# Sliding-window attention and a two-layer feed-forward on one core: chunk 1's first layer ahead of chunk 0's second, two pairs of the third batch in tiles, V moved from two queues, and the last batch transposed on TensorE

## The chip, the cores and the metric

The kernel runs on one core of a Trainium2 chip. The metric is the device time of one execution in microseconds (us). An execution that was taken with a profile also shows its span, from the first to the last instruction of the core.

## The reference

q, k and v have the shape batch 8, heads 8, sequence 576, head size 64. Each position attends to itself and to the 63 positions before it. The result, 4,608 tokens of 512 values, goes through two matrices with `h - tanh(h)` between them. Cut to what is computed:

```python
scores = scale * np.matmul(q, k.transpose(0, 1, 3, 2))       # scale = 1/8
rel = pos[:, None] - pos[None, :]
mask = (rel >= 0) & (rel < 64)
scores = np.where(mask, scores, -1e9)
attn = np.exp(scores - np.max(scores, axis=-1, keepdims=True))
attn = attn / (np.sum(attn, axis=-1, keepdims=True) + 1e-9)
x = np.matmul(attn, v).transpose(0, 2, 1, 3).reshape(4608, 512)
h = x @ w_in                                                  # 512 x 2048
return (h - np.tanh(h)) @ w_out                               # 2048 x 512
```

## The kernel before, in words

**Attention.** Two heads make a pair; pair number g runs from 0 to 31, four to a batch (g = 4 x batch + pair). A sequence is cut into nine windows of 64 queries; each window looks at 128 keys, its own 64 and the 64 before. For each pair:

- q and k are loaded with a cast to bf16 (`load`, `load_all`; these DMAs are issued by POOL) and copied into rows in which the two heads lie side by side (`cast`, line 86, on VectorE or POOL).
- TensorE transposes them into PSUM, six transposes for each of q and k, and copies bring them to `qT` (or `qs`) and `kT`. There are two buffers of each (`g % NR`).
- The *wide* form (`tr`, `scores`, `masking`, `pv`, `norm`, lines 259 to 358) keeps q of the two heads in separate columns, with zeros in the other head's rows, so `qT` must have been cleared. ScalarE takes the exponential, VectorE multiplies with the mask, TensorE multiplies with V (which carries a column of ones, so the row sums come along), and VectorE divides.
- The *tile* form (`tr_rows`, `hides`, `tile_scores`, `tile_pv`, lines 278 to 324) works on half the rows of the array for each head. The mask is added by matmuls that write large negative numbers ahead of the scores (`hides`), and no mask is multiplied later. It needs one copy each for q and k.

Batches 0 and 1 use the tile form, batches 2 to 7 the wide one. V is loaded as 72 rows of eight positions, cast into `vb` (`cast_v`) and moved by nine DMAs to `vw`, in which window j has its 64 keys on the upper partitions (`keys_v`, or `windows_v` for both halves); `shift_dve` or `shift_v` copies them to the lower half of the next window. `vb` is single, `vw` is double.

In batch 7 of the kernel before, TensorE doesn't transpose q and k. POOL copies q to zeroed rows (`cast_q` to `qz`, cleared by `more_zeros`), SP writes q and k to DRAM (`bounce`) and reads them back with transposing DMAs into `qT` and `kT` (`tr_dma`).

The results of a batch, in `xs`, are transposed to `xT`, on TensorE (`x_tr`, half 0 or 1 being the pairs 0, 1 or 2, 3) up to batch 3, and by transposing DMAs (`x_dma`, SP) from batch 4 on.

**Feed-forward.** The 4,608 tokens are nine chunks of 512. A chunk has eight windows and a batch nine, so chunk c needs the batches up to c. For each of 16 slices m of 128 hidden units `hp_mm` runs four matmuls of 512 columns (line 396), ScalarE takes tanh (401), and VectorE subtracts into `gT` (`g_sub`, 408). The second layer, `yp_mm` (420), has 16 groups of four matmuls too: group st is a quarter of the sum for the 128 tokens s = st // 4. After four groups ScalarE copies the bank out (`y_out`, 425) and SP stores it. The first layer uses PSUM banks 0 to 2 for its first groups and then 0 and 1; the second layer uses bank 2, and in the last chunk banks 0 and 2.

**What sets the order.** The order on each engine is written by hand and kept. The program runs over slots h. A slot may hold one group of the feed-forward (table `OPS`), and anything else is hung on a slot by `at(h, fn, ...)`:

```python
OPS[2 * m] = "h", 0, m
OPS[32 + 2 * m] = "h", 1, m
OPS[49 + 2 * m if m < 8 else 56 + m] = "y", 0, m
for c in range(2, NC + 1):
    if c < NC:
        OPS[32 * c + 8 + 2 * m] = "h", c, m
    OPS[32 * c + 9 + 2 * m] = "y", c - 1, m
```

In a slot the group's matmuls come first, then what hangs on the slot, then the subtraction of the group. A slot costs no time by itself. Each engine takes its own instructions in this order, and one that waits holds up all behind it. For a pair in the wide form a number a (`STEPS`, or a formula) sets its places: casts of q and k at a - 7 and a - 5, transposes at a and a + 2, scores at a + 5, a + 7 and a + 9, mask at a + 11, products with V at a + 13 to a + 15, norm at a + 15. `LOADS` holds the slots of the loads of a batch (k, q, V) and `VALUES` those of V's casts and moves. Before each of these loads, POOL copies one element of the newest `gT` (`pace`, the `tick` of line 453), which keeps it from running ahead.

DMAs issued by POOL share eight completion semaphores in turn, so that one waits until the eighth before it has landed. Row buffers for casts are three deep for q and for k, `vall` is single, `qall` and `kall` are double.

Ahead of the loop stand batch 0 and the loads of batch 1's pairs and of `w_in`. `w_out` is loaded from slot 27.

Of the kernel before, what the change touches and what calls it, by code (L numbers as in the profile page):

```python
# [15 lines left out]
def kernel(  # L16
# [9 lines left out]
    nc = tc.nc  # L26
# [24 lines left out]
    dram = ctx.enter_context(tc.tile_pool(name="dram", bufs=2, space=bass.MemoryType.DRAM))  # L51
# [24 lines left out]
    qz = [const.tile([P, 2, E, 128], BF16, name=f"qz{i}") for i in range(2)]  # L76
# [40 lines left out]

    def cast_q(g):

        i = stage.pop((g, "q")).rearrange("p h (e d) -> p h e d", d=D)  # L120
        for h in range(2):
            nc.gpsimd.tensor_copy(qz[g % 2][:, h, :, 64 * h:64 * h + 64], i[:, h])

    def bounce(g, n):

        if n == "q":
            t = dram.tile([2, S, 128], BF16, tag="q", name="qd")
            nc.sync.dma_start(out=t.rearrange("h (p e) c -> p h (e c)", e=E),
                              in_=qz[g % 2].rearrange("p h e c -> p h (e c)"))
        else:  # L130
            t = dram.tile([S, 128], BF16, tag="k", name="kd")
            nc.sync.dma_start(out=t.rearrange("(p e) c -> p (e c)", e=E),
                              in_=rows.pop((g, "k")).rearrange("p e h d -> p (e h d)"))
        rows[g, n + "d"] = t

    def tr_dma(g, n):
        t = rows.pop((g, n + "d"))
        if n == "q":
            nc.sync.dma_start(out=qT[g % NR].rearrange("c h s -> c (h s)"),
                              in_=t.rearrange("h s c -> (h s) c"), transpose=True)  # L140
        else:
            nc.sync.dma_start(out=kT[g % NR][:, 64:], in_=t, transpose=True)
# [89 lines left out]

    def more_zeros(i):
        nc.gpsimd.memset(qz[i], 0.0)
# [175 lines left out]
    def yp_bank(c, s):  # L410
        if c == 0:
            return 2
        return (0, 2)[s % 2] if c == NC - 1 else 2
# [16 lines left out]
    for m in range(M):  # L430
        OPS[2 * m] = "h", 0, m
        OPS[32 + 2 * m] = "h", 1, m
        OPS[49 + 2 * m if m < 8 else 56 + m] = "y", 0, m
        for c in range(2, NC + 1):
            if c < NC:
                OPS[32 * c + 8 + 2 * m] = "h", c, m
            OPS[32 * c + 9 + 2 * m] = "y", c - 1, m
# [89 lines left out]
    at(6, lambda: [cast_v(1, pr, V) for pr in range(NP)])  # L527
    at(7, lambda: [keys_v(1, j, (G, Y)[j % 2]) for j in range(NJ)])
    at(7, load_v_all, 2)
    for g in 8, 9, 10, 11:  # L530
        at(7, load, g, "k", G)
        at(7, load, g, "q", G)
    at(9, cast_pair, 4, V)
    at(11, cast_pair, 5, V)
    at(18, cast_pair, 6, V)
    at(20, cast_pair, 7, V)
    at(22, shift_dve, 1, 0, 4)
    for g, t, ka, qa, a, b in ((4, (11, 12, 13, 14), 6, 7, (4, 5), (6, 7)), (5, (14, 15, 15, 15), 2, 3, (4, 5), (6, 7)),
                             (6, (19, 20, 21, 22), 2, 3, (4, 5), (4, 5)), (7, (21, 22, 24, 25), 2, 3, (4, 5), (4, 5))):
        at(t[0], tr_rows, g, "k", ka, V)  # L540
# [3 lines left out]
    for pr in range(NP):  # L544
        at(24 + 2 * pr, tile_pv, 4 + pr, (6, 7))
    at(26, lambda: [cast_v(2, pr, V) for pr in range(NP)])
    at(27, lambda: nc.vector.memset(qT[1], 0.0))
    at(29, x_tr, 1, 0, 0, 4, 3, A)
    at(30, x_tr, 1, 0, 4, 9, 4, A)
    at(31, x_tr, 1, 1, 0, 4, 3, V)  # L550
    at(31, x_tr, 1, 1, 4, 9, 4, A)
    at(27, lambda: [keys_v(2, j, G) for j in range(NJ)])
    at(27, load_w_out, 0)
    at(27, load_w_out, 1)
    at(27, load_all, 3, "q")
# [109 lines left out]
```

The softmax here doesn't subtract the row's maximum and nothing guards it: scores larger than these inputs give would overflow.

## Time and profile before

| what | value |
|---|---|
| median of 13 runs | 366.15 us (361.32 to 369.68) |
| the profiled execution's own time | 366.46 us |
| its span | 364.7 us |
| mean granted TensorE clock in it | 0.956 |
| TensorE matmuls, busy | 326.2 us, 2,380 recorded |
| VectorE, ScalarE, POOL, busy | 202.9, 184.5, 104.3 us |
| first layer, line 396 | 576 matmuls, 152.2 us busy |
| second layer, line 420 | 576 matmuls, 145.8 us busy |
| DMA | 41.84 MB, 115 GB/s in the mean |

The busy time of a matmul in the profile contains its way through the array, so neighbours overlap; how long a group of matmuls keeps the engine is read from the distance of the starts, or from the chain of work that ended last. A row in order of time has its start, its duration, the engine, the line and the operation, the tiles, the number of instructions merged, and in brackets the idle time of the engine before it with what ended this. A row of the windows has the stretch, its length, and busy time and count of PE, its weight loads (PEld), VectorE (DVE), ScalarE (ACT) and POOL, then the granted clock, the busy share of the DMA engines and their GB/s.

### The profile page before, as it was taken

The numbers are of one execution on the slowest core, as the hardware profiler recorded it, in microseconds if no ns is written. First come the engines' busy times: TensorE is split into PE (matmuls) and PEld (weight loads), VectorE is DVE, ScalarE is ACT, GpSimd is POOL, SyncE is SP. The second block draws the span as 40 slices with busy tenths as digits, with TensorE's granted clock in tenths as the row PEclk, the third lists the DMA queues.
The fourth block names the chain that finished last, engine by engine and source line by source line (L and its number), as shares of the span: only waits on it lengthen the run. The fifth ranks groups of instructions, "written<-read, shape, count | busy, mean of one in ns | idle before, by whom it ended". The sixth has DMA issues, their size and how long they took to land.

```text
span 364.7 us, 6139 instructions
## 1 busy us (share of the span) xinstructions
PE 326.2 (89%) x2380; PEld 178.3 (49%) x2380; DVE 202.9 (56%) x340; ACT 184.5 (51%) x336; POOL 104.3 (29%) x153
## 2 busy tenths in 40 slices
PE   6787785799879997999999999598999999999995
PEld 2553454355435554555555555154455444444442
DVE  4566578687534676567666686255556443344300
ACT  3533664656526564665656656254554443443421
POOL 8913707206104164652272260701000000000000
PEclk9559999889999999999999999899999999999999
DMA  8999985993059938946796779458940410011012
GB/s 160 161 193 179 167 126 66 175 202 81 29 101 153 154 64 141 148 89 107 161 150 140 139 112 133 115 132 179 200 131 31 94 54 33 29 42 45 30 59 85
DMA packets 50006, 41.84 MB, mean 115 GB/s; under 512 B 20873, under 2 KB 43337, under 8 KB 49785
## 3 DMA queue, kind: packets, MB, share of 16 engines
q0 software_dynamic: 21248, 19.34, 36.1%
q1 hardware_dynamic: 28376, 21.69, 26.0%
q10 hardware_dynamic: 352, 0.43, 0.4%
q8 instruction: 18, 0.29, 0.3%
q14 instruction: 12, 0.09, 0.1%
HBM read 36.70 MB, written 11.21 MB: 131 GB/s over the span
## 4 chain that ended last, share of the span: by engine, by line
PE 64%; DVE 10%; issue 8%; ACT 7%; DMA 6%; POOL 4%; ACTq 0%; SPq 0%; DVEq 0%; POOLq 0%
PE ps L420 28%; PE ps L396 26%; PE ps L346 3%; DVE xs L357 2%; PE ps L330 2%; DVE gT L408 2%; DMA w_out_sb<-in_moe_w_out_dram 2%; DMA kt<-kd 2%; DVE qt L86 2%; DMA vall<-in_v_dram 2%; ACT qt L84 1%; ACT th L401 1%; PE ps L263 1%; PE ps L363 1%; ACT pt L305 1%
## 5 line engine op out<-in xcount | busy, mean ns | idle before, releaser
L396 PE MATMUL ps<-xT,wi 128*128 128x512 bf16 x576 | 152.2, 389 | 3.6 <-DVE gT L408 2.0
L408 DVE TENSOR_TENSOR gT<-ps,th 128x512 bf16<-128x512 f32 x144 | 98.7, 690 | 96.9 <-ACT th L401 95.3
L420 PE MATMUL ps<-w_out_sb,gT 128*128 128x512 bf16 x576 | 145.8, 381 | 2.9 <-ACT ysb L425 2.8
L401 ACT ACTIVATE th<-ps 128x512 f32<-128x512 f32 x144 | 85.8, 598 | 92.1 <-PE ps L396 91.0
L396 PEld LDWEIGHTS <-wi 128*128 128x128 bf16 x576 | 61.4, 115 | 51.4 <-issue 8.3
L420 PEld LDWEIGHTS <-gT 128*128 128x128 bf16 x576 | 54.0, 98 | 58.0 <-issue 5.0
L332 ACT ACTIVATE pt<-ps 128x384 bf16<-128x384 f32 x72 | 35.2, 490 | 38.9 <-PE ps L330 38.8
L357 DVE TENSOR_TENSOR xs<-ps,rc 64x576 bf16<-64x576 f32 x48 | 36.2, 755 | 1.2
L425 ACT ACTIVATE ysb<-ps 128x512 f32<-128x512 f32 x36 | 21.5, 597 | 17.2 <-PE ps L420 17.2
L86 DVE COPY qt<-ps 64x576 bf16<-64x576 bf16 x20 | 15.2, 760 | 21.6 <-ACT qt L84 21.6
L86 POOL COPY vb<-vall 72x1024 bf16<-72x1024 bf16 x20 | 20.8, 1056 | 22.6 <-DMA vall<-in_v_dram 21.0
L346 PEld LDWEIGHTS <-pt 128*128 128x128 bf16 x216 | 18.2, 99 | 18.4 <-DVE pt L336 2.5
L330 PE MATMUL ps<-qt,kt 128*128 128x128 bf16 x216 | 24.3, 222 | 1.8 <-DMA kt<-kd 1.8
L346 PE MATMUL ps<-vw,pt 128*128 128x130 bf16 x216 | 24.2, 223 | 1.6 <-DVE pt L336 1.6
L86 POOL COPY qb<-qall 96x768 bf16<-96x768 bf16 x16 | 13.3, 828 | 29.6 <-DMA qall<-in_q_dram 25.1
L330 PEld LDWEIGHTS <-kt 128*128 128x128 bf16 x216 | 16.7, 99 | 9.9 <-DMA kt<-kd 2.2
L336 DVE TENSOR_TENSOR pt<-pt,ps 128x1152 bf16<-128x1152 bf16 x24 | 17.9, 745 | 0.1
L86 POOL COPY kb<-kall 96x768 bf16<-96x768 bf16 x20 | 16.6, 832 | 2.0 <-ACT pt L332 2.0
L84 ACT ACTIVATE kt<-ps 128x576 bf16<-128x576 bf16 x20 | 13.0, 650 | 7.7 <-PE ps L263 7.7
L176 POOL DMA_DIRECT2D vw<-vb x19 | 12.2, 655 | 11.7 <-DVE gT L408 8.1
L263 PE MATMUL ps<-ident,kb 96*128 96x96 bf16 x120 | 8.6, 209 | 6.3 <-POOL kb L86 4.3
L84 ACT ACTIVATE qt<-ps 64x576 bf16<-64x576 bf16 x20 | 12.7, 633 | 0.3 <-PE ps L263 0.3
(73 smaller groups left out, 193.4 us busy)
## 6 DMA issues: line engine op xcount, KB each, us to landing
out_dram<-ysb SPq DMA_DIRECT2D x36, 256.0 KB
vall<-in_v_dram POOLq DMA_DIRECT2D x7, 576.0 KB, 10.5
qall<-in_q_dram POOLq DMA_DIRECT2D x5, 576.0 KB, 9.7
kall<-in_k_dram POOLq DMA_DIRECT2D x5, 576.0 KB, 8.6
vw<-vb SPq DMA_DIRECT2D x35, 65.0 KB
vw<-vb SPq DMA_DIRECT2D x16, 130.0 KB
wi<-in_moe_w_in_dram POOLq DMA_DIRECT2D x2, 1024.0 KB, 15.5
w_out_sb<-in_moe_w_out_dram POOLq DMA_DIRECT2D x2, 1024.0 KB, 12.4
```

What stands on the lines that cost most here:

```text
L84: nc.scalar.activation(o, i, ACT.Copy)
L86: eng.tensor_copy(o, i)
L330: nc.tensor.matmul(sp[:, i, :], kT[g % NR][:, 64 * j:64 * j + 128], qT[g % NR][:, :, 64 * j:64 * j + 64], start=True, stop=True)
L332: nc.scalar.activation(PT[g % NPT][:, 3 * grp:3 * grp + 3, :], sp, ACT.Exp, scale=scale)
L336: nc.vector.tensor_tensor(p, p, mask.unsqueeze(1).to_broadcast([128, 2 * NJ, 64]), ALU.mult)
L346: nc.tensor.matmul(ps[:, 5 + grp, 130 * i:130 * i + 130], PT[g % NPT][:, j, :], vw[b % 2][:, j, 2 * pr:2 * pr + 2, :], start=True, stop=True)
L357: nc.vector.tensor_tensor(xo[r, :, :, pr, :], ov[r, :, :, h, 0:D], rc[r].to_broadcast([64, 3, 3, 64]), ALU.mult)
L396: nc.tensor.matmul(hp, w_in_tile(ki, m), chunk_tile(c)[:, :, ki % 2, 64 * (ki // 2):64 * (ki // 2) + 64], start=(ki == 0), stop=(ki == 3))
L401: nc.scalar.activation(th, hp, ACT.Tanh)
L408: nc.vector.tensor_tensor(gT[c][:, m, :], hp, th, ALU.subtract)
L420: nc.tensor.matmul(yp, gT[c][:, m, s * 128:(s + 1) * 128], w_out_sb[:, m, :], start=(m == 0), stop=(m == M - 1))
L425: nc.scalar.activation(ysb, ps[:, yp_bank(c, s), :], ACT.Copy)
```

## The change

The edit has four parts and what follows from them:

- The second layer of chunk 0 goes to slots 64 to 79, one group to a slot, behind all of chunk 1's first layer, and uses PSUM banks 0 and 1 in turn. Everything from chunk 2 on stands eight slots later. The first group of each chunk takes half 0 of its input before half 1.
- Batch 1's steps among slots 6 to 31 are respaced: casts of pairs 4 and 5 stand before V's cast, which goes from slot 6 to 11 (with its moves and the loads behind them from 7 to 12). k of pairs 6 and 7 is copied by ScalarE instead of VectorE.
- Pairs 8 and 9 of batch 2 use the tile form, at slots 29 to 48, among chunk 1's first layer. V of batch 2 and pairs 8 to 11 are cast by POOL instead of VectorE; V's moves for batch 2, and for batch 3, are issued by POOL and SP in turn. `w_out` is loaded from slot 23.
- Batch 7 is treated as batches 3 to 6: q and k are cast by POOL at a - 7 and a - 5 and transposed on TensorE. `qz`, `cast_q`, `bounce`, `tr_dma` and `more_zeros` go.

The diff, cut to its core:

```diff
-    qz = [const.tile([P, 2, E, 128], BF16, name=f"qz{i}") for i in range(2)]
...
     def yp_bank(c, s):
         if c == 0:
-            return 2
+            return s % 2
         return (0, 2)[s % 2] if c == NC - 1 else 2
...
-        OPS[49 + 2 * m if m < 8 else 56 + m] = "y", 0, m
+        OPS[64 + m] = "y", 0, m
         for c in range(2, NC + 1):
             if c < NC:
-                OPS[32 * c + 8 + 2 * m] = "h", c, m
-            OPS[32 * c + 9 + 2 * m] = "y", c - 1, m
+                OPS[32 * c + 16 + 2 * m] = "h", c, m
+            OPS[32 * c + 17 + 2 * m] = "y", c - 1, m
...
-    at(6, lambda: [cast_v(1, pr, V) for pr in range(NP)])
-    at(7, lambda: [keys_v(1, j, (G, Y)[j % 2]) for j in range(NJ)])
-    at(7, load_v_all, 2)
+    at(3, lambda: nc.vector.memset(qT[1], 0.0))
+    at(8, cast_pair, 4, V)
+    at(9, cast_pair, 5, V)
+    at(11, lambda: [cast_v(1, pr, V) for pr in range(NP)])
+    at(12, lambda: [keys_v(1, j, (G, Y)[j % 2]) for j in range(NJ)])
+    at(12, load_v_all, 2)
     for g in 8, 9, 10, 11:
-        at(7, load, g, "k", G)
-        at(7, load, g, "q", G)
-    at(9, cast_pair, 4, V)
-    at(11, cast_pair, 5, V)
-    at(18, cast_pair, 6, V)
-    at(20, cast_pair, 7, V)
-    at(22, shift_dve, 1, 0, 4)
-    for g, t, ka, qa, a, b in ((4, (11, 12, 13, 14), 6, 7, (4, 5), (6, 7)), (5, (14, 15, 15, 15), 2, 3, (4, 5), (6, 7)),
-                             (6, (19, 20, 21, 22), 2, 3, (4, 5), (4, 5)), (7, (21, 22, 24, 25), 2, 3, (4, 5), (4, 5))):
-        at(t[0], tr_rows, g, "k", ka, V)
+        at(12, load, g, "k", G)
+        at(12, load, g, "q", G)
+    at(16, cast_pair, 6, V)
+    at(18, cast_pair, 7, V)
+    at(21, shift_dve, 1, 0, 4)
+    for g, t, ka, qa, a, b, eng in ((4, (10, 11, 13, 14), 6, 7, (4, 5), (6, 7), V),
+                                    (5, (13, 14, 15, 15), 2, 3, (4, 5), (6, 7), V),
+                                    (6, (17, 18, 20, 21), 2, 3, (4, 5), (4, 5), A),
+                                    (7, (19, 20, 23, 24), 2, 3, (4, 5), (4, 5), A),
+                                    (8, (29, 30, 34, 36), 3, 2, (4, 5), (4, 5), A),
+                                    (9, (36, 37, 41, 43), 3, 2, (4, 5), (4, 5), A)):
+        at(t[0], tr_rows, g, "k", ka, eng)
         at(t[1], tr_rows, g, "q", qa, A)
...
-        at(24 + 2 * pr, tile_pv, 4 + pr, (6, 7))
-    at(26, lambda: [cast_v(2, pr, V) for pr in range(NP)])
-    at(27, lambda: nc.vector.memset(qT[1], 0.0))
-    at(29, x_tr, 1, 0, 0, 4, 3, A)
-    at(30, x_tr, 1, 0, 4, 9, 4, A)
-    at(31, x_tr, 1, 1, 0, 4, 3, V)
+        at(22 + 2 * pr, tile_pv, 4 + pr, (6, 7))
+    at(27, x_tr, 1, 0, 0, 4, 3, A)
+    at(28, x_tr, 1, 0, 4, 9, 4, A)
+    at(30, x_tr, 1, 1, 0, 4, 7, V)
     at(31, x_tr, 1, 1, 4, 9, 4, A)
-    at(27, lambda: [keys_v(2, j, G) for j in range(NJ)])
-    at(27, load_w_out, 0)
-    at(27, load_w_out, 1)
-    at(27, load_all, 3, "q")
-    at(27, load_all, 3, "k")
-    at(27, load_v_all, 3)
-    at(41, shift_dve, 2, 0)
-    at(42, shift_dve, 2, 4)
-    at(100, more_zeros, 0)
-    at(116, more_zeros, 1)
+    at(21, lambda: [cast_v(2, pr) for pr in range(NP)])
+    at(22, cast_pair, 8, G)
+    at(23, lambda: [keys_v(2, j, (G, Y)[j % 2]) for j in range(NJ)])
+    at(23, load_w_out, 0)
+    at(23, load_w_out, 1)
+    at(23, load_all, 3, "q")
+    at(23, cast_pair, 9, G)
+    at(23, load_all, 3, "k")
+    at(23, load_v_all, 3)
+    at(24, cast_pair, 10, G)
+    at(38, cast_pair, 11, G)
+    at(40, shift_dve, 2, 0, 4)
+    at(43, tile_pv, 8, (6, 7))
+    at(48, tile_pv, 9, (6, 7))
+    at(51, x_tr, 2, 0, 0, 4, 4, V)
+    at(52, x_tr, 2, 0, 4, 9, 5, A)
+    at(76, x_tr, 2, 1, 0, 4, 3, V)
+    at(78, x_tr, 2, 1, 4, 9, 3, A)
...
-    LOADS = {4: (74, 75, 77), 5: (101, 104, 97), 6: (132, 136, 119), 7: (156, 160, 150)}
-    STEPS = {2: (30, 38, 46, 54), 3: (63, 70, 77, 84), 4: (91, 98, 105, 112), 5: (119, 126, 134, 142)}
-    XTR = {9: (58, 60), 11: (70, 71), 13: (88, 90), 15: (100, 102)}
-    VALUES = {3: (64, 1, 68), 4: (84, 1, 90), 5: (107, 2, 115), 6: (124, 5, 142), 7: (156, 5, 174)}
-    for g in range(2 * NP, B * NP):
+    LOADS = {4: (75, 77, 79), 5: (106, 109, 102), 6: (140, 144, 126), 7: (168, 171, 158)}
+    STEPS = {2: (0, 0, 49, 58), 3: (72, 79, 86, 93), 4: (100, 107, 114, 121), 5: (128, 135, 142, 149)}
+    TURNS = {13: (97, 3, 99, 3), 15: (110, 4, 111, 3)}
+    VALUES = {3: (66, 1, 71), 4: (88, 1, 93), 5: (110, 2, 120), 6: (132, 5, 150), 7: (164, 5, 182)}
+    for g in range(2 * NP + 2, B * NP):
         b, pr = divmod(g, NP)
-        a = STEPS[b][pr] if b in STEPS else 8 * g - 44
-        if b == 2:
-            at((28, 33, 41, 49)[pr], cast_pair, g, V)
-        elif b == 7:
-            at(a - 14, cast_q, g)
-            at(a - 13, cast, g, "k")
-            at(a - 12, bounce, g, "q")
-            at(a - 11, bounce, g, "k")
-            at(a - 6, tr_dma, g, "q")
-            at(a - 5, tr_dma, g, "k")
-        else:
+        a = STEPS[b][pr] if b in STEPS else 8 * g - 36
+        if b > 2:
             at(a - 7, cast, g, "q")
             at(a - 5, cast, g, "k")
-        if b < 7:
-            at(a, tr, g, "q", 2 if g < 10 else 3, A, V)
-            at(a + 2, tr, g, "k", 2 if g < 10 else 3, A)
+        at(a, tr, g, "q", 2 if g < 13 else 3, A, V)
+        at(a + 2, tr, g, "k", 3, A)
...
-                at(ky + j // 2, windows_v if b < 5 else keys_v, b, j, Y)
+                if b == 3:
+                    at(ky, windows_v, b, j, (G, Y)[j % 2])
+                else:
+                    at(ky + j // 2, windows_v if b < 5 else keys_v, b, j, Y)
...
-                hp_mm(c, (m,), False)
+                hp_mm(c, (m,), m == 0)
```

## The prediction

> **What bounds the kernel now.** I read the page's busy shares and slices first, then PE's own rows in order of time, the windows, and last POOL's rows. Two groups run through the whole span, L396 (first layer) and L420 (second). At full clock four matmuls of either take 0.864 us in the chain of work that ended last, so 1,152 of them need 249 us.
>
> From the page (shares; slices of 9.1 us each):
>
> ```profile
> PE 326.2 (89%) x2380; PEld 178.3 (49%) x2380; DVE 202.9 (56%) x340; ACT 184.5 (51%) x336; POOL 104.3 (29%) x153
> ...
> PE   6787785799879997999999999598999999999995
> ...
> PEclk9559999889999999999999999899999999999999
> ```
>
> PE is the bound, and it has holes only in slices 0 to 15 and 24 to 28: from about 264 us on it never waits. The windows (time, PE busy, other engines, granted clock, DMA) put numbers to the stages:
>
> ```profile
> 26.50:63.20 36.70, 27.44 (x308) 15.22 (x307) 25.57 (x52) 19.82 (x36) 17.39 (x27) 0.97 0.92 136
> 63.20:79.70 16.50, 13.82 (x91) 7.69 (x90) 11.67 (x20) 9.96 (x19) 3.04 (x4) 0.80 1.07 185
> 79.70:109.60 29.90, 25.96 (x196) 14.62 (x193) 16.65 (x28) 13.77 (x26) 8.77 (x10) 1.00 0.42 81
> 109.60:228.50 118.90, 113.71 (x856) 65.13 (x853) 78.08 (x123) 73.82 (x141) 48.00 (x65) 1.00 0.80 130
> 228.50:264.00 35.50, 29.37 (x176) 15.49 (x177) 17.74 (x28) 16.01 (x29) 9.58 (x15) 0.95 0.72 154
> 264.00:361.00 97.00, 96.95 (x478) 47.62 (x476) 38.75 (x58) 39.81 (x68) 0.00 (x0) 1.00 0.18 58
> ```
>
> Summing the bracketed idle times of PE's rows gives 9.3 us (26.5 to 62.5), 3.8 (to 79.7), 4.2 (to 110.2), 4.9 (to 228.5) and 6.2 (to 264). The clock of 0.80 over 16.5 us costs 3.3 more. The late part in PE's rows:
>
> ```profile
> 227.45 1.03 PE L396 MATMUL ps<-xT,wi 128*128 128x512 bf16 x4
> 232.79 0.43 PE L263 MATMUL ps<-ident,kb 96*128 96x96 bf16 x6 [4.32 <-POOL kb L86]
> 233.06 1.24 PE L420 MATMUL ps<-w_out_sb,gT 128*128 128x512 bf16 x4
> 234.10 1.91 PE L396 MATMUL ps<-xT,wi 128*128 128x512 bf16 x4
> ...
> 254.55 0.34 PE L330 MATMUL ps<-qt,kt 128*128 128x128 bf16 x3 [1.03 <-DMA kt<-kd]
> 263.44 0.34 PE L330 MATMUL ps<-qt,kt 128*128 128x128 bf16 x3 [0.80 <-DMA kt<-kd]
> ```
>
> and its cause in POOL's rows: the q of the last batch is copied far ahead (for the bounce through DRAM), waits for its load, and the k of the pair before stands behind it:
>
> ```profile
> 217.03 0.83 POOL L86 COPY qb<-qall 96x768 bf16<-96x768 bf16 x1
> 230.01 0.96 POOL L122 COPY qz<-qall 96x384 bf16<-96x384 bf16 x2 [12.16 <-DMA qall<-in_q_dram]
> 230.91 1.06 POOL L86 COPY vb<-vall 72x1024 bf16<-72x1024 bf16 x1
> 231.91 0.83 POOL L86 COPY kb<-kall 96x768 bf16<-96x768 bf16 x1
> ```
>
> **What the skill says.** The Trainium skill, "TensorE: Matmul & The Clock Gate", Part 1: The HAM clock gate, says that PE falls to half clock after an idle window of some 3.4 us and needs as long to come back. The trace agrees: after the 4.32 us hole the next groups of four took 1.08, 1.71 and 1.49 us, 1.7 us lost. "DMA: Bandwidth & Descriptors", Issuing engines are not separate DMA queues, says that a second issuing engine saves only issue time; here nine moves of V took POOL 5.2 us to issue, so four of them on SP are worth 2.3 us of POOL. "SBUF — State Buffer", Who interferes with whom, says that VectorE copies can lock GpSimd out; POOL's first three moves from 34.17 us took 0.99 us each beside such copies, against 0.58 later.
>
> **The change part by part.** Slots are the loop's h.
>
> *(1) Slots 0 to 31 (chunk 0 with batch 1), respaced.* Work is the same. I followed the new order by hand with the durations of the rows (first layer 0.864, tanh 0.60, subtraction 0.69, transposes of a pair 0.26, reciprocal and product 1.05). The wait for a k copy (1.74 at 35.39) goes, for the copies now stand ahead of V's; four waits for qs (0.70, 0.47, 0.69, 0.36) mostly shrink, as a first-layer group now lies between; waits before the x transposes and chunk 1's first group (1.10, 0.52, 0.97, 1.11) shrink to about 1.2. Together some 5.5 us less.
>
> Against it: V of batch 1 is cast five slots later (about 38.4 us instead of 33.9), so POOL issues its five moves to about 42, and load V of batch 2 at 42.5 instead of 39.09. In before:
>
> ```profile
> 39.09 0.84 POOL L146 DMA_DIRECT2D vall<-in_v_dram  x1 [0.26 <-DMA qall<-in_q_dram]
> ...
> 48.08 0.63 POOL L97 DMA_DIRECT2D qall<-in_q_dram  x1 [3.36 <-DMA vall<-in_v_dram]
> 56.77 1.20 POOL L176 DMA_DIRECT2D vw<-vb  x2 [8.06 <-DVE gT L408]
> 58.24 4.03 POOL L176 DMA_DIRECT2D vw<-vb  x7 [0.28 <-issue]
> 62.20 1.54 POOL L199 DMA_DIRECT2D w_out_sb<-in_moe_w_out_dram  x2
> ```
>
> The last load waited for V's landing (9.0 us after issue), so now about 51.2 to 51.9. Then POOL, no longer VectorE, casts V (4 x 1.05 = 4.2, to 56.1), k and q of pair 8 (2 x 0.83, to 57.8), five moves (3, to 61), w_out (1.5, to 62.5: as late as before), q of batch 3 (0.9), pair 9 (to about 66). PE comes to pair 8's k at about 54 and waits to 57.0, 2.9 us. Net: chunk 1's first group ends at 60.6 instead of 63.2, with one more transposition done: **-2.6 us**.
>
> *(2) Slots 32 to 79.* Work of PE from there to chunk 2's first group (109.6 in before): 15 + 16 groups x 0.864 = 26.8; ten transpositions x 0.26; scores and products of twelve-odd groups x 0.17 = 4.4; x transposes 1.0: 34.8 us. Before spent 46.4: it lost 8.0 in idle time and 3.3 to the clock. After does 35.7: one transposition fewer, and per tiled pair 0.6 more (hiding matmuls 0.6, 18 of 64 columns 0.54, 20 of 65 columns 0.46, against two times 0.51). Two bank waits go, 1.33 and 0.52 (the second layer of chunk 0 now alternates two banks, which the first layer has left), and so does most of the 2.35 before chunk 2 (1.01 + 0.42 + 0.66 + 0.26: three second-layer groups now lie between the norm and the x transposes). VectorE loses two pairs' masks and half-products, 2.2 us each, which are hidden by PE. New: pair 9's casts end at 65 to 66 while PE is there at 63.6: 2.3. ScalarE carries about 17.7 us of rows in 22 us of slots 32 to 63; I allow 1.0. The clock gate is the unknown: from 0 (no window idle enough) to 7 (four such windows of 1.7); I take two, 3.4. w_out lands 12.4 us (median) after issue, about 75 to 77, and slot 64 comes at about 82: hidden by chunk 1's groups; without these it would cost up to 14.5, the slower load. Sum 42.4 against 46.4: **-4.0 us**.
>
> *(3) Slots 80 on, up to batch 7.* Eight slots later as a whole. Loads, casts and moves keep their distances or gain some; SP and POOL pass the same instructions. Batch 3's last x transposes get one slot more: of 2.28 + 0.35 + 0.15, about 1 stays: **-1.8 us**.
>
> *(4) Batch 7 on TensorE.* Removed: q's copy to zeroed rows (8 x 0.52), its two clears (2 x 1.38), 16 DMAs of SP. The hole of 4.32, its clock loss of 1.7 and the two waits for kt (1.03, 0.80) go: -7.9. Added on PE: 8 x 6 transposes = 8 x 0.26 = +2.1. Added on ScalarE 4 x (0.63 + 0.65), on VectorE 4 x 0.76: hidden by PE's groups, as in batches 3 to 6. The first q is now cast 7 slots ahead of its use, not 22. But k and q still land about 17 us after k's issue (212.83 to 230.0), which V's cast delays to about slot 171: q is there at about slot 187.5, cast by 188.5, needed at 188. Between 0 and 2 us; I take +1. **-4.8 us**.
>
> Sum: -2.6 - 4.0 - 1.8 - 4.8 = -13.2. The profiled execution took 366.46 us (span 364.7 and 1.8 around it), so 353.3; the median of the runs is 0.3 lower: **353.0 us**.
>
> **Rivals.**
> *A, as worked out*: 353, own range 347 to 358. *B, POOL becomes the early bound*: casts of V, pairs 8 to 11, moves and w_out hang one behind another; if POOL's copies are locked out as at 34.17 (0.99 against 0.58) the chain of some 14 us grows by half, 7 us, PE waits at pairs 8 and 9 for all of it, and (1) and (2) give nothing: 360. For it: POOL was idle 8.06 us there and now isn't. Against: VectorE has fewer copies of its own then. *C, the late hole stays*: the loads of batch 7 were moved three to four slots nearer to their use, too; if q lands after slot 191, PE waits 4 or more and the clock falls: 353 + 5 = 358. *D, better*: no clock window lost, POOL copies on time, hence -6: 347. *E, slower*: V of batch 2 lands late. Its load stands behind moves that now wait for a cast at slot 11, and everything in (1) up to w_out waits for it in POOL's queue. Each us beyond 51 is paid once by PE; it decides from 13 us on (landing after 64, 22 us after issue). The slowest V load of this trace took 20.9, but with w_out and two others ahead, and here there is none: 371.
>
> **How the numbers follow.** A 0.50, B 0.22, C 0.10, D 0.11, E 0.07. A, B, C and D are faster by over 0.5% (about what a measurement of this kernel can tell from no change, 1.8 us), save a part of B that goes on to 364 to 368: 0.05. Hence faster 0.88, same 0.05, slower 0.07. The range, 345 to 362, holds A, D and most of B and C, with both ends of the clock (-3.4, +3.4) and POOL.
>
> **What would show it.** PE's rows: no wait for a bounced kt, and one under 2 us for the first q of batch 7; no wait for ysb in chunk 0's second layer; chunk 2's first group at about 103 us instead of 109.6; idle before pair 8's k and pair 9's k and q of 2 to 3 us each, released by POOL. Wrong if POOL's row of V's first cast starts after 55, if the clock is near half from 54 to 82, if PE waits for w_out at slot 64, or if the late hole has only moved to another pair.

## The result, and the profile after

The changed kernel takes 348.94 us (median of 11 runs, 347.93 to 349.75), the kernel before 365.03 (median of 48 runs on several chips, 360.76 to 369.68). The ratio of the two, taken from runs beside each other, is 0.958, with a 95% interval of 0.955 to 0.960: 15.3 us less. (The medians themselves are 16.1 apart; that of before takes in runs on other chips.) The forecast was 353.0 with a range of 345 to 362. The profiled execution took 349.03 us, 17.4 less than that of before, which was itself 1.4 above its median; its span is 347.0, 17.7 less.

The busy shares and the slices (8.7 us each) on the page of the changed kernel:

```profile
PE 322.8 (93%) x2476; PEld 178.8 (52%) x2476; DVE 197.4 (57%) x324; ACT 189.0 (54%) x344; POOL 111.9 (32%) x160
...
PE   6678896888999999999999999999999999999995
...
PEclk9558999999999999999999999999999999999999
```

Counted from 0, slices 24 to 28, the second hole of before, are full, and so is the clock behind the start. What is left is slices 0 to 9. The windows, cut near the events that answer to those of before (the start of chunk 1's first layer, its last wait, the first group of chunk 2, the start of the late stretch):

```profile
26.50:60.90 34.40, 28.48 (x323) 16.14 (x322) 22.23 (x45) 22.04 (x40) 19.69 (x29) 0.97 0.97 146
60.90:84.80 23.90, 19.99 (x205) 11.59 (x203) 16.55 (x25) 16.28 (x30) 9.98 (x12) 1.00 0.98 169
84.80:101.20 16.40, 16.40 (x118) 8.85 (x116) 6.09 (x10) 5.92 (x13) 14.46 (x22) 1.00 0.61 99
101.20:218.00 116.80, 114.52 (x869) 66.21 (x867) 79.70 (x125) 74.52 (x143) 47.38 (x63) 1.00 0.75 135
218.00:250.00 32.00, 32.00 (x237) 18.41 (x235) 21.67 (x35) 20.68 (x39) 2.58 (x4) 1.00 0.33 79
```

PE now never waits from 84.8 to 101.2, where chunk 0's second layer stands, nor after 218, and the clock is full in both. Its bracketed waits sum to 5.9, 3.8, 0, 2.2 and 0 us in these five windows. PE's rows show where the early ones are:

```profile
56.58 0.43 PE L252 MATMUL ps<-ident,kb 96*128 96x96 bf16 x6 [2.35 <-POOL kb L84]
...
58.47 0.59 PE L365 MATMUL ps<-xT,wi 128*128 128x512 bf16 x2
59.49 1.46 PE L365 MATMUL ps<-xT,wi 128*128 128x512 bf16 x6 [0.42 <-ACT xT L82]
...
63.25 0.43 PE L252 MATMUL ps<-ident,kb 96*128 96x96 bf16 x6 [0.30 <-POOL kb L84]
64.02 0.43 PE L252 MATMUL ps<-ident,qb 96*128 96x96 bf16 x6 [0.33 <-POOL qb L84]
...
81.44 0.42 PE L232 MATMUL ps<-ident,kb 96*128 96x96 bf16 x6
83.42 1.02 PE L365 MATMUL ps<-xT,wi 128*128 128x512 bf16 x4 [1.56 <-DVE gT L377]
...
101.23 1.03 PE L365 MATMUL ps<-xT,wi 128*128 128x512 bf16 x4
```

The six matmuls at 59.49 are the last two of chunk 1's first group and the four of its second; one takes 0.216 us, so the first group ends at 59.9. The first window above, to 60.9, thus holds one group more than that of before, to 63.2, but no further wait. In PE's rows of before:

```profile
62.47 0.94 PE L396 MATMUL ps<-xT,wi 128*128 128x512 bf16 x3 [1.11 <-DVE xT L86]
63.20 0.69 PE L263 MATMUL ps<-ident,kb 96*128 96x96 bf16 x6
```

A wait costs more than its bracket, which counts from the modelled end of the matmul before. The six transposes at 81.44 keep PE for 0.26 us and the next group starts at 83.42, so PE lost 1.72 us, not 1.56. By this row each wait costs about 0.16 us more than is shown (an estimate).

The wait at 56.58 is for pair 8's k, and POOL's rows show that it hangs on the load of V of batch 2, as step (1) had it. The last load issue below waits for V's landing, 9.5 us after its issue, and then four casts of V stand ahead of pair 8's k:

```profile
41.59 0.86 POOL L118 DMA_DIRECT2D vall<-in_v_dram  x1
...
51.10 0.63 POOL L95 DMA_DIRECT2D qall<-in_q_dram  x1 [4.19 <-DMA vall<-in_v_dram]
51.73 4.03 POOL L84 COPY vb<-vall 72x1024 bf16<-72x1024 bf16 x4
55.71 0.82 POOL L84 COPY kb<-kall 96x768 bf16<-96x768 bf16 x1
```

Late, in POOL's rows, q of batch 7 is there long before PE first transposes it, at 223.03:

```profile
206.08 0.77 POOL L101 DMA_DIRECT2D qall<-in_q_dram  x1
...
214.24 0.83 POOL L84 COPY qb<-qall 96x768 bf16<-96x768 bf16 x1 [3.80 <-DMA qall<-in_q_dram]
```

The load landed 8 us after issue. In the kernel before it took 14.7.

Stage by stage, from the two profiled executions:

| stage | before | after | difference | forecast |
|---|---|---|---|---|
| end of chunk 1's first group | 63.2 | 59.9 | -3.3 | -2.6 |
| from there to chunk 2's first group | 46.4 | 41.3 | -5.0 | -4.0 |
| from there to the last second-layer run | 236.55 | 227.07 | -9.5 | -6.6 |
| from there to the end of the span | 18.6 | 18.7 | +0.1 | 0 |

The third stage holds steps (3) and (4). Its waits up to the late stretch fell from 4.9 to 2.2 us (-2.7, forecast -1.8). In the late stretch 6.2 us of waits and 1.7 of clock went and 2.1 of transposes came (-5.8, forecast -4.8). The remaining 1.0 us is in no bracket; the stage has six waits instead of twelve, and six times the 0.16 above would make it up.

### The profile page after: what moved, and what is told of

It is laid out like the page before. It is cut to its first block, busy times and chain, and to the rows that moved or that the text cites. A ratio compares the mean times of both kernels' runs of the same rounds, so it can differ in the third digit from the quotient of the medians.

```text
span 347.0 us, 6309 instructions
## 1 busy us (share of the span) xinstructions
PE 322.8 (93%) x2476; PEld 178.8 (52%) x2476; DVE 197.4 (57%) x324; ACT 189.0 (54%) x344; POOL 111.9 (32%) x160
## 4 chain that ended last, share of the span: by engine, by line
PE 74%; DVE 7%; DMA 6%; POOL 5%; ACT 4%; issue 2%; ACTq 0%; DVEq 0%; POOLq 0%
PE ps L389 35%; PE ps L365 29%; PE ps L315 3%; PE ps L299 3%; DMA qall<-in_q_dram 3%; PE ps L232 3%; DVE gT L377 2%; DMA vw<-vb 2%; DMA vall<-in_v_dram 2%; POOL vw L148 1%; DVE xs L326 1%; PE ps L332 1%; POOL vb L84 1%; DVE qt L84 1%; DVE vw L154 1%
## 5 line engine op out<-in xcount | busy, mean ns | idle before, releaser
L365 PE MATMUL ps<-xT,wi 128*128 128x512 bf16 x576 | 148.1, 381 | 4.3 <-DVE gT L377 3.7
L301 ACT ACTIVATE pt<-ps 128x384 bf16<-128x384 f32 x66 | 32.3, 490 | 25.5 <-PE ps L299 25.5
L84 POOL COPY vb<-vall 72x1024 bf16<-72x1024 bf16 x24 | 24.8, 1055 | 39.0 <-DMA vall<-in_v_dram 28.2
L326 DVE TENSOR_TENSOR xs<-ps,rc 64x576 bf16<-64x576 f32 x44 | 33.2, 755 | 1.1
L84 POOL COPY qb<-qall 96x768 bf16<-96x768 bf16 x24 | 20.4, 852 | 27.1 <-DMA qall<-in_q_dram 22.5
L315 PEld LDWEIGHTS <-pt 128*128 128x128 bf16 x198 | 16.5, 98 | 14.7
L299 PE MATMUL ps<-qt,kt 128*128 128x128 bf16 x198 | 21.8, 219 | 0.0
L84 POOL COPY kb<-kall 96x768 bf16<-96x768 bf16 x24 | 20.5, 852 | 1.3 <-PE ps L232 1.3
L82 ACT ACTIVATE kt<-ps 128x576 bf16<-128x576 bf16 x26 | 16.9, 649 | 3.8 <-PE ps L252 2.0
L274 ACT ACTIVATE pt<-ps 128x640 bf16<-128x640 f32 (+1 forms) x20 | 12.6, 648 | 5.3 <-PE ps L271 5.3
L148 POOL DMA_DIRECT2D vw<-vb x16 | 9.6, 612 | 7.4 <-DVE vb L84 6.6
```

Of the source, the lines that this page charges most:

```text
L82: nc.scalar.activation(o, i, ACT.Copy)
L84: eng.tensor_copy(o, i)
L299: nc.tensor.matmul(sp[:, i, :], kT[g % NR][:, 64 * j:64 * j + 128], qT[g % NR][:, :, 64 * j:64 * j + 64], start=True, stop=True)
L301: nc.scalar.activation(PT[g % NPT][:, 3 * grp:3 * grp + 3, :], sp, ACT.Exp, scale=scale)
L315: nc.tensor.matmul(ps[:, 5 + grp, 130 * i:130 * i + 130], PT[g % NPT][:, j, :], vw[b % 2][:, j, 2 * pr:2 * pr + 2, :], start=True, stop=True)
L326: nc.vector.tensor_tensor(xo[r, :, :, pr, :], ov[r, :, :, h, 0:D], rc[r].to_broadcast([64, 3, 3, 64]), ALU.mult)
```

## The experiments

Each kernel is the changed one with the edit shown, except the first. The ratio is to the kernel before, run beside it on the same chip; the changed kernel's is 0.958. A difference of 0.001 is 0.37 us. Kernels that ran on different chips are compared by their ratios, since the median of before lay between 363.2 and 366.8. In the profiled executions the start differs for reasons that are not in the edits (the clock rises or `w_in` lands earlier or later; the first scores of pair 4 start between 34.6 and 38.0 us), so rows are compared over stretches behind it.

### Batch 7 on TensorE, alone in the kernel before

```diff
-            at(a - 14, cast_q, g)
-            at(a - 13, cast, g, "k")
-            at(a - 12, bounce, g, "q")
-            at(a - 11, bounce, g, "k")
-            at(a - 6, tr_dma, g, "q")
-            at(a - 5, tr_dma, g, "k")
...
-        if b < 7:
-            at(a, tr, g, "q", 2 if g < 10 else 3, A, V)
-            at(a + 2, tr, g, "k", 2 if g < 10 else 3, A)
+        at(a, tr, g, "q", 2 if g < 10 else 3, A, V)
+        at(a + 2, tr, g, "k", 2 if g < 10 else 3, A)
```

The casts at a - 7 and a - 5, that batches 3 to 6 have, now hold for batch 7 too; loads and slots stay.

> The kernel before with one part of the change: q and k of batch 7 cast by POOL at a - 7 and a - 5 and transposed on TensorE, loads of batch 7 where they were. My theory: the late hole (4.32 us, 1.7 of clock) and the two waits for kt (1.03, 0.80) go and 2.1 us of transposes come: 5.8 us less, about 359.5. Rival, that the way through DRAM was hidden and only the transposes count: 2 us more, about 367.

Measured: 359.93 us, ratio 0.982 (0.978 to 0.986), 6.4 us less. The late hole is gone although the load is as slow as before: q was issued at 216.78 and landed at 231.6, 14.8 us later. In POOL's rows of this kernel:

```profile
231.61 0.82 POOL L86 COPY qb<-qall 96x768 bf16<-96x768 bf16 x1 [9.50 <-DMA qall<-in_q_dram]
```

POOL still waits here, but what stands behind it is no longer due. In the kernel before, a cast that stood 19 slots ahead of the first scores that use it held back one that stood seven ahead of its transposition. So step (4) is shown by itself, and its size (-5.8 without the late q) lies within the interval of this run, 5 to 8 us.

### The reverse: batch 7 through DRAM again, in the changed kernel

The edit is the one above the other way round (`cast_q`, `bounce`, `tr_dma`, their tiles and two clears restored for batch 7).

> The changed kernel with batch 7 going through DRAM as before, q copied at a - 14. If the bounce as such costs PE 5.8 us: about 354.7. My theory, that the hole came from POOL's order together with a q that landed 14.7 us after issue, while in the changed kernel it lands 8.0 us after issue (214.2, just before PE comes to the k of the pair before, 216.7): the hole does not come back, waits for kt of 1 to 2 us do, and 2.1 us of transposes go: 348 to 350.

Measured: 350.99 us, ratio 0.955 (0.951 to 0.960): no difference from the changed kernel that these runs can tell. The hole does not come back; two waits for kt (1.48 at 240.51 and 0.27 at 248.87) and one of 0.55 for V do, against 2.1 us of transposes saved. q landed 7.8 us after issue here. The same edit is worth 6.4 us in one order and nothing measurable in the other. The two runs with the other pairings agree on why: a late cast behind a slow load (the run before) makes no hole, an early cast behind a fast load (this one) makes none, and only the kernel before has both an early cast and a slow load.

### What a late q would cost: casts early, then a collision

```diff
-            at(a - 7, cast, g, "q")
-            at(a - 5, cast, g, "k")
+            at(a - (14 if b == 7 else 7), cast, g, "q")
+            at(a - (13 if b == 7 else 5), cast, g, "k")
```

> The changed kernel with one edit: the casts of batch 7 stand at a - 14 (q) and a - 13 (k), transposes stay on TensorE. If an early cast of q by itself makes the hole: 4 to 6 us more, about 354. If it takes an early cast and a late landing: q lands at about 214.2, behind it pass 3 to 4 POOL copies, so PE waits at most 1 us at 216.7: 349 to 350.

The second kernel has this and moves batch 5's transposing DMAs towards the loads:

```diff
-            at(a + 16, x_dma, b)
+            at(a + (21 if b == 5 else 16), x_dma, b)
```

> As the run with early casts, and batch 5's x transposes (SP) five slots later, so that they run beside the loads of k and q of batch 7 as they did before. If their sharing the DMA engines made q land 14.7 us after issue instead of 8.0, q lands at about 221 and PE waits about 5 to 6 us for the k of pair 27, and the clock drops: 355 to 357. If the x transposes have no part in it: the same as with early casts alone.

Measured: 349.45 us, 0.953 (0.950 to 0.957) for the first, with no new wait; 349.95, 0.954 (0.951 to 0.958) for the second. By time the two can't be told apart, and the 355 to 357 us of a full hole did not come. But only the second has a wait there, in PE's rows:

```profile
218.74 0.43 PE L232 MATMUL ps<-ident,kb 96*128 96x96 bf16 x6 [1.27 <-POOL kb L84]
```

It is the mechanism of the hole, a k behind a q that waits for its load, and a quarter of the size. The q took 9.45 us from issue to landing, against 7.4 in the first kernel. The transposing DMAs started at 202.76 and took 4.1 us, so they were nearly over when q was issued at 206.65; in the kernel before they started together with the k load, at 212.85, and took 5.3. (There both hang on slot 156; in the changed kernel the transposing DMAs hang on slot 164 and the k load on 168.) That they make the load slow is likely from this. That they account for all of 14.7 against 8.0 us is not shown.

### Chunk 0's second layer: its place and its banks

First both undone, then the banks alone. With bank 2 taken by the second layer, all q of the wide pairs must be transposed in bank 3, beside k, in both kernels.

```diff
-            return s % 2
+            return 2
...
-        OPS[64 + m] = "y", 0, m
+        OPS[49 + 2 * m if m < 8 else 56 + m] = "y", 0, m
...
-        at(a, tr, g, "q", 2 if g < 13 else 3, A, V)
+        at(a, tr, g, "q", 3, A, V)
```

> The changed kernel with chunk 0's second layer back among chunk 1's first (slots 49 to 71, bank 2). Theory: w_out lands 12 to 14 us after its issue at 60.1, about 72 to 75, when slot 49 comes, so little is waited for it; but three waits for the copy of the one bank come back (1.33, 0.52, 0.4 in the kernel before), and slots 72 to 79 hold only attention steps, so chunk 2's first group follows its x transposes without cover (2.4): 4 us more, about 353. Rival, that the order of the two layers carries none of the gain: within 1 us of 348.9.

Without the edit of `OPS`:

> The changed kernel with chunk 0's second layer on bank 2 alone, order unchanged. Theory: at slots 68, 72 and 76 PE waits for the bank's copy, 0.5 to 1.3 us each as in the kernel before: 1.5 to 3.5 us more, about 351. Rival: attention steps between cover it: under 0.5.

Measured: 355.23 us, 0.981 (0.974 to 0.988), and 354.01, 0.974 (0.969 to 0.980). Both cost more than expected, 8 and 6 us by the ratios, and the two can't be told apart by time. From chunk 1's second group on, the profiled executions are 6.8 and 3.5 us longer than that of the changed kernel. The first kernel's own part shows in its rows where chunk 2 begins:

```profile
102.45 0.61 PE L332 MATMUL ps<-ident,xs 128*128 128x128 bf16 x4 [1.40 <-DVE xs L326]
```

With 0.26 and 0.53 behind it this makes 2.2 us of waits, where 2.4 were expected, and the clock is 0.50 from 102 to 108.7. PE's rows of the second kernel:

```profile
79.12 0.41 PE L232 MATMUL ps<-ident,kb 96*128 96x96 bf16 x6 [0.99 <-DVE qt L84]
...
93.70 3.61 PE L389 MATMUL ps<-w_out_sb,gT 128*128 128x512 bf16 x16 [1.07 <-ACT ysb L394]
```

Four waits for the copy of the bank (1.07, 0.52, 0.69, 0.47) make 2.75 us, the expected part. The waits of 0.99 and 0.96 for qt come from bank 3 being shared by q and k, that is from the side condition of the experiment and not from the banks of the second layer; against them, 0.31 is left of the 1.56 us before chunk 1's last group. In its profiled execution pair 8's k also came 0.6 later and the clock fell behind it, before the second layer begins. So two banks in turn are worth 2.75 us by the rows. The place is measured only with one bank in both kernels: the step from the second to the first costs 3.3 us by the rows (6.8 against 3.5) and 2 by the ratios, which is within their noise. The place with two banks kept was not measured.

### Pairs 8 and 9 in the wide form

```diff
-                                    (8, (29, 30, 34, 36), 3, 2, (4, 5), (4, 5), A),
-                                    (9, (36, 37, 41, 43), 3, 2, (4, 5), (4, 5), A)):
...
-    STEPS = {2: (0, 0, 49, 58), 3: (72, 79, 86, 93), 4: (100, 107, 114, 121), 5: (128, 135, 142, 149)}
+    STEPS = {2: (29, 36, 49, 58), 3: (72, 79, 86, 93), 4: (100, 107, 114, 121), 5: (128, 135, 142, 149)}
...
-    for g in range(2 * NP + 2, B * NP):
+    for g in range(2 * NP, B * NP):
```

> The changed kernel with pairs 8 and 9 in the wide form, at a = 29 and 36, x transposes of half 0 at 54 and 56. PE has 1.2 us less work, VectorE 4.4 us more in 30 us, ScalarE about the same. Theory: the tile form is worth little on PE; VectorE's longer norm and mask add some waits: -1 to +2, about 349.5. Rival, that the tiles carry a good part of the early gain: 3 us or more above.

Measured: 351.89 us, 0.968 (0.964 to 0.973), 3.8 us above the changed kernel by the ratios. PE has less work in this kernel and waits more, above all for VectorE:

```profile
68.90 0.51 PE L315 MATMUL ps<-vw,pt 128*128 128x130 bf16 x6 [1.76 <-DVE pt L305]
```

The mask's multiplication (`pt`) comes late, with further waits of 0.94, 1.56 and 1.24 for subtractions of VectorE. Step (2) charged the tile form with 1.2 us of PE for two pairs, and called the 4.4 us that VectorE saves hidden. They are not, at least where this run puts the wide pairs: from chunk 1's second group to chunk 2's first PE takes 44.6 us instead of 41.3.

### Who casts and who moves V of batch 2

VectorE casts V of batch 2 and pairs 8 to 11, as in the kernel before:

```diff
-    at(21, lambda: [cast_v(2, pr) for pr in range(NP)])
-    at(22, cast_pair, 8, G)
...
-    at(23, cast_pair, 9, G)
...
+    at(26, lambda: [cast_v(2, pr, V) for pr in range(NP)])
+    at(28, cast_pair, 8, V)
...
+    at(33, cast_pair, 9, V)
```

> The changed kernel with V of batch 2 and pairs 8 to 11 cast by VectorE at slots 26, 28, 33, 45, 53, and V's moves, w_out and batch 3's loads at slot 27. Theory: the wait of 2.35 us before pair 8's k (POOL) shrinks to about 1, those at pair 9 (0.3 and 0.3) go, VectorE has 4.2 us more and makes first-layer groups wait for banks, 1 to 2 us; w_out is issued 1 to 2 us later, which is covered: -1 to +1.5, about 349. Rival, that POOL's casts carry the gain: 3 us or more above.

All nine moves of V of batch 2 on POOL:

```diff
-    at(23, lambda: [keys_v(2, j, (G, Y)[j % 2]) for j in range(NJ)])
+    at(23, lambda: [keys_v(2, j, G) for j in range(NJ)])
```

> The changed kernel with all nine moves of batch 2's V issued by POOL, not by POOL and SP in turn. In the changed kernel the five that POOL issues keep it from 57.25 to 60.1 us, 0.58 us each, between pair 8's q and w_out. If the second queue carries a part of the gain, four more of 0.58 put w_out, pair 9's casts and batch 3's first q 2.3 us later: pair 9's k at about 65, PE's waits there grow from 0.63 to 2 to 3 us, and the time is 1 to 2.5 us above the changed kernel's (ratio to the kernel before about 0.962 to 0.965, about 350.5 us). Rival: pair 9's k has slack behind the hiding matmuls and the next groups; then 0.3 us or less is lost (ratio 0.958).

Measured: 347.33 us, 0.956 (0.950 to 0.961), and 352.84, 0.967 (0.960 to 0.975). The engine of the casts carries nothing that these runs can tell: with VectorE the wait at pair 8's k is 2.29, released by VectorE. It casts V in 1.42 us instead of 4.03, but comes to it at 52.6, 2.6 us after V's landing, and pair 8's k is ready at 55.9, as with POOL at 56.5. With one queue the ratio is 3.4 us above that of the changed kernel, with an interval from 0.5 to 6. PE's rows of this kernel:

```profile
59.06 0.66 PE L252 MATMUL ps<-ident,kb 96*128 96x96 bf16 x6 [2.93 <-POOL kb L84]
59.52 1.91 PE L365 MATMUL ps<-xT,wi 128*128 128x512 bf16 x4
...
67.94 0.43 PE L252 MATMUL ps<-ident,kb 96*128 96x96 bf16 x6 [1.31 <-POOL kb L84]
```

Pair 9's k and q now cost 1.31 + 0.33 instead of 0.63, by the mechanism expected, and the clock falls behind them: it was 0.72 from 68 to 74 us. Pair 8's wait of 2.93 and the clock behind it (0.73 from 56 to 62; the group at 59.52 starts 1.70 us before what follows it, twice 0.86) don't belong to the edit, since POOL comes to the moves only after pair 8's casts and V's load took 10.1 us in this execution, not 9.5. From chunk 1's second group to chunk 2's first this kernel takes 43.1 us, the changed one 41.3. These 1.8 us lie in the range expected; that the second queue carries more than its 2.3 us of issue time is not shown.

### The load of V of batch 2, earlier

A second buffer for the loaded rows, with the load and pair 8's ahead:

```diff
-    v_pool = ctx.enter_context(tc.tile_pool(name="v", bufs=1))
+    v_pool = ctx.enter_context(tc.tile_pool(name="v", bufs=2))
...
-    at(12, load_v_all, 2)
+    at(4, load_v_all, 2)
...
-        at(12, load, g, "k", G)
-        at(12, load, g, "q", G)
+        at(4 if g == 8 else 12, load, g, "k", G)
+        at(4 if g == 8 else 12, load, g, "q", G)
```

> The changed kernel with a second buffer for the loaded V rows, so that V of batch 2 needn't wait for the casts of batch 1's: its load and those of pair 8's q and k are issued at slot 4 instead of 12. My step (1) holds that PE's wait of 2.35 us at pair 8's k comes from this late load (issued 41.6, landed 51.1) through POOL's queue of casts. If so, V lands before 45, POOL's casts are done when PE comes, and the waits of 2.35 and 0.63 (pairs 8 and 9) go: -2 to -3 us against the changed kernel, about 346 (ratio 0.949 to 0.953). Rival: the earlier load only delays the loads it now stands ahead of (batch 1's later pairs, the w_in slices), or POOL's queue is held by the moves and not by the load: within 1 us of the changed kernel, with new waits in slots 4 to 20.

Or the one buffer freed earlier, by casting V of batch 1 on POOL:

```diff
-    at(11, lambda: [cast_v(1, pr, V) for pr in range(NP)])
-    at(12, lambda: [keys_v(1, j, (G, Y)[j % 2]) for j in range(NJ)])
-    at(12, load_v_all, 2)
+    at(4, lambda: [cast_v(1, pr) for pr in range(NP)])
+    at(4, load_v_all, 2)
+    at(4, lambda: [keys_v(1, j, (G, Y)[j % 2]) for j in range(NJ)])
...
-        at(a, tr, g, "q", 2 if g < 13 else 3, A, V)
+        at(a, tr, g, "q", 2 if g < 13 else 3, A, V) if g != 11 else at(a, tr_vector_first, g)
```

The clears of `vw[1]` and `qT[1]` go to POOL as well and the loads of pairs 8 to 11 to slot 5. `tr_vector_first` is `tr` for q with the two copies in the other order.

> The changed kernel with V of batch 1 cast by POOL at slot 4 instead of VectorE at slot 11 (POOL was idle from 31.7 to 38.3 us), so that V of batch 2 is loaded some 4 us earlier without a second buffer; two clears go to POOL, and in pair 11 VectorE copies its half of q without waiting for ScalarE's. If the late V load sets the wait at pair 8's k, that wait falls from 2.35 to about 0.5; the wait of 1.56 us at 83.42 (VectorE's subtraction behind its copy of q, which waited for ScalarE's) falls to about 0.2; VectorE has 2.4 us less to do: -3 to -5 us against the changed kernel, about 345 (ratio 0.945 to 0.950). Rival: the casts on POOL are slowed beside VectorE's copies (0.99 against 0.58 per move was seen there) and delay batch 1's own q and k casts: no gain, waits in slots 8 to 20 instead.

Measured: 346.59 us, 0.950 (0.945 to 0.955), and 346.56, 0.953 (0.945 to 0.960). With two buffers the wait at pair 8's k is gone, and of pair 9's 0.63 there is 0.33. V lands 13.0 us after its issue, not 9.5, but at 45.3 instead of 51.1. In POOL's rows:

```profile
32.23 0.85 POOL L118 DMA_DIRECT2D vall<-in_v_dram  x1
...
45.27 0.67 POOL L95 DMA_DIRECT2D kall<-in_k_dram  x1 [2.81 <-DMA vall<-in_v_dram]
```

This settles step (1): at the same speed of POOL the wait goes with the load. New waits of 0.42, 0.79 and 0.32 for V of batch 1, whose moves now stand behind the load, cost part of it, so that the rows show a net gain of 1.0 us behind the first scores of pair 4. The other 1.5 us between the two profiled executions lie ahead of these scores (34.62 against 36.10), where the clock rose some 2.6 us earlier. The ratios give 2.9 us, with an interval from 0.8 to 5. In the second kernel the wait at pair 8's k is gone too, but the gain of 3 to 5 us that was expected did not come. PE waits 2.15 us for pair 4's k, for a cast of VectorE that took 2.55 us instead of 0.34. VectorE's and POOL's rows:

```profile
30.46 4.03 POOL L84 COPY vb<-vall 72x1024 bf16<-72x1024 bf16 x4
32.15 2.55 DVE L84 COPY kb<-kall 96x768 bf16<-96x768 bf16 x1
```

VectorE's copy ends just after POOL's four, and the three casts that follow it took 0.34 or 0.35. That was the rival's direction turned round: VectorE is held up by POOL, not POOL by VectorE.

### Two buffers, and pair 11's copies exchanged

```diff
+        move(nc.vector, o[64:128, 1], t[64:128])
+        move(nc.scalar, o[0:64, 0], t[0:64])
...
-        at(a, tr, g, "q", 2 if g < 13 else 3, A, V)
+        at(a, tr, g, "q", 2 if g < 13 else 3, A, V) if g != 11 else at(a, tr_vector_first, g)
```

> The kernel with two buffers for the loaded V rows (346.6 us), and in pair 11 VectorE copies its half of q before ScalarE's instead of after it. Theory: PE's wait of 1.56 us before chunk 1's last first-layer group is the sum of two copies that run one behind the other in front of a subtraction of VectorE; with the order exchanged it was 0.52 in the run that also moved V's casts. Then this kernel is 1 us faster than with two buffers alone: about 345.5 us, ratio to the kernel before 0.946 to 0.950, with waits of 0.4 us or less at the k of pairs 8 and 9 and about 0.5 before chunk 1's last group. Rival: the wait only moves to pair 11's scores or to chunk 2's first second-layer groups: within 0.3 us of two buffers alone.

The wait at 83.42 in the changed kernel comes from VectorE's copy of q, which waits for ScalarE's copy of the other half and holds up the subtraction behind it. The rows of VectorE, of the changed kernel:

```profile
81.89 0.76 DVE L84 COPY qt<-ps 64x576 bf16<-64x576 bf16 x1 [1.56 <-ACT qt L82]
82.68 0.69 DVE L377 TENSOR_TENSOR gT<-ps,th 128x512 bf16<-128x512 f32 x1
```

Measured: 344.77 us, 0.946 (0.943 to 0.950), as expected. The wait before chunk 1's last group is 0.45 instead of 1.56, and none comes in its place. (The profiled execution is the slowest of the seven, 347.36: the clock was at half from 51.1 to 54.5 us, behind waits of 0.46, 0.86 and 0.33 for V of batch 1.) By time alone the exchange can't be told from two buffers without it, since the intervals touch; the rows show it. This kernel is 1.2% (about 4 us) faster than the changed one, and the fastest of all that were run.

## Why the prediction was right

The sign, the range and most of the mechanisms held; the time was 4 us better than the likeliest case and lies between rivals A and D. Point by point, by the steps:

- *Step (1), -2.6, measured -3.3.* Right in kind. The waits other than pair 8's fell by 5.7 us, where 5.5 was forecast. For pair 8 the forecasts, with the measured times in brackets, were: POOL's load of V at 42.5 (41.6), landing 51.2 to 51.9 (51.1), pair 8's k ready at about 57 (56.5), PE's wait 2.9 (2.35). The runs with an earlier load confirm the cause of pair 8's wait. Batch 1's new order, which the 5.7 us come from, was not taken out by itself.
- *Step (2), -4.0, measured -5.0.* Four terms were mis-sized. The clock was put at 3.4 us lost and lost none in this execution. Pair 9's casts were put at 2.3 and cost 0.63, since the hiding matmuls and scores of pair 8 and a first-layer group stood between. ScalarE was allowed 1.0, and the other waits came to 3.2, of which 1.56 is the pair of copies of pair 11. PE's own work, the 41.3 us less the bracketed waits, was 37.5 us, not 35.7; seven waits at 0.16 above their brackets would be 1.1 of these 1.8. Together -3.4 - 1.7 + 2.2 + 1.8 = -1.1, the whole difference. The sentence that VectorE's two masks are "hidden by PE" is refuted by the wide form's run (+3.8), but this error left the sum unchanged, for no gain had been booked for it. The step's bank waits (1.33 and 0.52) were right in kind: put back on one bank, 2.75 us of them returned.
- *Why step (2) did not notice that its 35.7 was short.* Its parts for before, 34.8 of work, 8.0 of idle time and 3.3 of clock, came near the 46.4 us measured. But the 8.0 count the wait of 1.11 ahead of the row at 62.47 a second time, which is in the 9.3 of the stretch before too, and 0.26 that lies behind the stage. The bracketed waits of that stretch are 6.6, so before's own work is 36.4 by the same reckoning, 1.6 more than 34.8.
- *Step (3), -1.8, measured -2.7.* Of the waits of 2.28, 0.35 and 0.15 at batch 3's last x transposes, where about 1 was to stay, 0.27 stayed. The step also said that loads keep their distances or gain some; it missed that q of batch 7 would land in 8 us instead of 14.7.
- *Step (4), -4.8, measured -5.8.* The +1 for a late q was wrong: k and q land 10 us after k's issue, not 17, and q is there about 8 us early. The 22 slots of the step run from the old cast to the new transposition. The rest stood by itself in the first experiment.
- The sum credits step (4) with a hole that is not there in the finished kernel, even with batch 7 through DRAM. The hole went either way, by the new casts or by the faster load, and the prediction counted it once, under the casts. That the total came out does not show that this part is needed: taken out of the finished kernel it is worth nothing that can be measured.

Of the rivals, B (POOL bound by lockout) is refuted: V's four casts took 4.03 us and five moves 2.86, neither stretched, and the casts' engine made no difference. Its neighbour, POOL bound by the load ahead of it, is what holds the 2.35 us. C is refuted by the row at 214.24. E did not occur: V landed after 9.5 us (for E's 371 us no working was given). D was right on the clock and nearly so on pair 9 (0.63), but pair 8's wait stayed.

The clock term deserves more than a miss. The Trainium skill, "TensorE: Matmul & The Clock Gate", Part 1: The HAM clock gate, says that PE's activity is watched over a window of some 3.4 us that runs freely. The traces agree: in each of them the granted clock changes only at times that lie whole multiples of 3.41 us apart (in before 63.07, 66.48, 73.31, 76.72, 233.74 and 237.15), so the windows can be laid through the places where nothing changed, too. Nine kernels have the wait at pair 8's first transposition:

| kernel | wait at pair 8 (us) | longest part of it in one window (us) | clock in the next window |
|---|---|---|---|
| changed kernel | 2.35 | 1.51 | stays full |
| second layer of chunk 0 between | 2.45 | 1.53 | stays full |
| pairs 8 and 9 wide | 2.67 | 1.77 | stays full |
| casts of batch 7 early | 2.73 | 1.80 | falls |
| casts on VectorE | 2.29 | 1.92 | falls |
| early casts, collision | 3.31 | 1.92 | falls |
| batch 7 through DRAM | 2.76 | 2.11 | falls |
| moves from one queue | 2.93 | 2.59 | falls |
| one bank | 2.99 | 2.88 | falls |

The length of the wait doesn't sort these cases (2.29 lost the clock, 2.67 kept it), the part in one window does. The page gives an idle window as what halves the clock; here a window that was idle for 1.80 of its 3.41 us was enough. This limit holds for this place only: elsewhere in the traces windows with 1.41, 1.64 and 1.67 us of bracketed idle time lost the clock and others with 1.62, 1.73 and 1.85 kept it, so idle time is not all that counts. Where the windows lie differs from one profiled execution to the next. An allowance was therefore right, and that the profiled execution lost nothing is luck.

A lost window also costs less than its length. In the run with early casts the clock was 0.50 from 56 to 62 us, 3 us of PE's work. But the waits of 0.42, 0.30, 0.33 and 0.47 that follow in the changed kernel were swallowed by it: from pair 8's k to the group that starts at 69.66 in the changed kernel it took 13.96 us instead of 13.08.

## What to carry to other kernels

When a wait is released by an engine that casts, look one row further up in that engine's queue: here a load, set by a single buffer, was the cause, and moving the casts to another engine changed nothing. Price what a stage saves on every engine that has little room there, not on the busiest alone: VectorE was busy for 16.6 of the 23.9 us from 60.9 to 84.8, and 4.4 us more of it cost 3.3 us of PE's time. Before summing up waits, lay each row into one stage only, and let the stages end at the same group in both kernels. And measure a part both alone in the old kernel and taken out of the new one before crediting it: the two answers were 6.4 us and nothing measurable.

## What was not expected of the hardware

- A VectorE copy of 96x768 bf16 that takes 0.34 us took 2.55 beside four POOL copies in a row, once: it did not get in between two of them. The Trainium skill, "SBUF — State Buffer", Who interferes with whom, says that whichever starts first holds the shared ports for the instruction and the other is blocked; here the block lasted past the ends of single copies (about 1.0 us each), to the end of all four.
- The load of q of batch 7, 576 KB, landed between 7.1 and 14.7 us after its issue in these traces. It was above 14 only where the transposing DMAs started together with the load ahead of it.
